# Moving the loads of the next tiles behind the read-back of rows, and the order of layer two's products, in a fused attention and mixture-of-experts kernel

## The chip, the cores and the metric

One NeuronCore of one Trainium2 chip runs the whole kernel. The metric is the device time of one execution in microseconds (us), taken as the median of several runs. A core has five instruction queues that matter here: TensorE (PE, matmuls and their weight loads), VectorE (DVE), ScalarE (ACT), GpSimd (POOL, which here only issues indirect DMAs) and SyncE (SP, which here only issues DMAs). Each queue runs its instructions in program order; an instruction that waits for a semaphore holds up all that stand behind it in its queue.

## The reference

```python
def attn(u, v, z):                       # u, v: (8, 2496, 256), z: (8, 2496, 64)
    scores = (1.0 / S) * (z @ z.transpose(0, 2, 1))
    return u * ((np.maximum(scores, 0.0) ** 2) @ v)

x = attn(u, v, z).reshape(19968, 256)
logits = x @ w_gate + modality_bias[modality_id]      # 8 experts
e_idx = logits.argmax(1)
gate_w = softmax(logits)[range(N), e_idx]
for e in range(8):                       # w1: (8, 256, 1024), w2: (8, 1024, 256)
    m = e_idx == e
    h = np.maximum(x[m] @ w1[e], 0.0)
    out[m] = gate_w[m, None] * (h @ w2[e])
```

## The kernel before

The first half of the time is the attention, which also computes each row's expert and scatters the rows to a DRAM buffer `xs`, sorted by expert. The second half is the mixture of experts, and only it is touched by the change. It works on tiles of 512 rows of one expert. There are 39 tiles that always run, numbered t = -4 to 34; t = -4 to -1 belong to one expert and share one set of weights, and from t = 0 on each tile reads its own expert's weights. Tiles -4 to 33 are "staged" (below); tile 34 and the rest after it take another path.

All products are made in float32r with operands split into a high and a low part, so that each product is three matmuls. A tile is computed in two halves of four slices of the hidden dimension (f = 0 to 3, then 4 to 7):

- `up` (L1356), for one slice f: six matmuls into one PSUM bank (L1365), then ACT writes the high part `hh` of the rectified result (L1369), and DVE the low part `hl` (L1370).
- `down` (L1434), after four `up`: 24 matmuls into two PSUM banks `po[0]` and `po[1]` (L1440). Sixteen take `hh` (with the high and the low part of the weights), and eight take `hl`.

So a tile is 96 matmuls of 128x512: 24 for four `up`, 24 for a `down`, and the same again. In `run_tile` the function `aside(f)` stands between these, and issues side work for other engines: after the first, second and fourth `up` and after the `down` of each half, as `aside(0)` to `aside(3)` and `aside(4)` to `aside(7)`.

The side work of a tile t is:

- Weights of tile t + 1. They arrive as four loads of 512 KB in buffers `wq` (L904); ACT casts each to a high part (L918) and DVE makes the low part (L922), one quarter in each of `aside(2)` to `aside(5)`. Seven buffers hold `wq`, so the last load for tile t + 2 needs the buffer that DVE's L922 of the first quarter of tile t + 1 reads.
- Rows of tile t + 1, which arrived as `xg` (four loads of 128 KB, L875) and `gate` (L877): DVE transposes them (`xt`, L941), ACT casts (`xh`, L948), DVE subtracts (`xl`, L953), in `aside(6)` and `aside(7)`. The second matmul of tile t + 1 reads `xl`.
- Results of tile t - 1. At the end of that tile `send` has DVE transpose the two banks (`squared`, L1452), and SP store them to a DRAM buffer (`stage`, L1456, four stores of 128 KB). The rest is put in a list `put_off`, with the step at which each is due: at `aside(2)` SP reads the tile back in another layout (`bring`, L1465, one load of 512 KB), and at `aside(4)`, `aside(5)`, `aside(6)` and `aside(6)` ACT multiplies a quarter of it by its gate (L1470), and POOL scatters that quarter to the output (L1389).

Loads for later tiles are issued on SP at the start of tile t, ahead of `run_tile(t)`: `prefetch(t)` issues the rows of tile t + 2 (L1632, which calls `fetch`, L859), and `fetch_weights(t + 2)` its weights (L1636, L890). SP's queue in a tile is therefore: the four stores of `stage` of the tile before, the rows of t + 2, the weights of t + 2, then `bring`.

Of the kernel before, what the change touches and what calls it, by code (L numbers as in the profile page):

```python
# [16 lines left out]
P = 128  # L17
# [5 lines left out]
def ins_of(x):  # L23
    return getattr(x, "ins", x)
# [3 lines left out]
def tile_attention_moe(ctx: ExitStack, tc: tile.TileContext, ut, v, zt, mid, wg, mb, w1, w2, out):  # L28
# [11 lines left out]
    nc = tc.nc  # L40
# [5 lines left out]
    KD, KF = D // P, F // P  # L46
# [9 lines left out]
    EARLY = min(4, (B - 1) * S // E // T)  # L56
    UNC = -(-N // T) - EARLY
# [51 lines left out]
    def iota_f32(shape, pattern, base, mult, name, pool=small):  # L109
        n = math.prod(shape[1:])  # L110
        i = raw.tile([P, n], I32, tag=name + "_i", name=name + "_i")
        f = pool.tile(shape, F32, name=name)
        nc.gpsimd.iota(i, pattern=pattern, base=base, channel_multiplier=mult)
        late.append((f, i))
        return f

    col = iota_f32([P, P], [[1, P]], 0, 0, "col", raw)
    part = iota_f32([P, 1], [[1, 1]], 0, 1, "part")
# [731 lines left out]
    def wait_rows(dmas):  # L850
        for s in scatters[ready["n"]:]:
            for i in dmas:
                tc.add_manual_dep(i, s.name, data, reason="rows of tokens")
        ready["n"] = len(scatters)

    def is_staged(t):
        return t < UNC - 1

    def fetch(t, r0=0, nj=J):  # L859

        n = t + EARLY
        cell = first[0:1, 1:2] if t < 0 else meta[0:1, t, 0:1]
        row = nc.sync.value_load(cell, min_val=0, max_val=(E - 1) * CAP if t < 0 else E * CAP - T)  # L863
        k = fetched["n"] % 2
        fetched["n"] += 1
        nt = nj * P
        xg = head[k].tile([P, T // BLK, KD * BLK], F32, tag=f"xg{k}", name="xg")[:, 0:nt // BLK, :]
        side = small.tile([P, J, 2], F32, tag="gate", bufs=4, name="gate")[:, 0:nj, :]
        r0 += n * T if t < 0 else 0
        src = xs[bass.ds(row + r0 if r0 else row, nt), :]  # L870
        dmas = []
        for b in range(P // BLK):
            cols = slice(b * KD * BLK, (b + 1) * KD * BLK)
            rows_of = src[:, cols].rearrange("(t i) c -> i t c", i=BLK)
            dmas.append(nc.sync.dma_start(out=xg[b * BLK:(b + 1) * BLK], in_=rows_of))  # L875
        order = "(p j) c -> p j c" if is_staged(t) else "(j p) c -> p j c"
        dmas.append(nc.sync.dma_start(out=side, in_=src[:, D:XW].rearrange(order, j=nj)))  # L877
        wait_rows([ins_of(i) for i in dmas])
        TL[t] = (side, xg)
# [7 lines left out]
    def weights_of(t):  # L887
        return W[0 if t < 0 else (t + 1) % NW]
# [27 lines left out]
    def part_weights_high(t, q):  # L916
        hi, _, x = quarter(t, q)
        nc.scalar.copy(out=hi, in_=x)  # L918

    def part_weights_low(t, q):  # L920
        hi, lo, x = quarter(t, q)
        nc.vector.tensor_tensor(out=lo, in0=x, in1=hi.bitcast(F32), op=ALU.subtract)  # L922
# [33 lines left out]
    def turn(t):  # L956
        for f in (turn_blocks, part_high, part_low):
            f(t)
# [20 lines left out]
    def piece(on, us, need, f, *args, after=(), take=(), drop=(), gate=-1):  # L979
        p = Piece(on, us, need, f, args, [d for d in (d if isinstance(d, tuple) else (d, 0.1) for d in after) if d[0]], list(take), drop, gate)  # L980
        pieces.append(p)
        return p
# [201 lines left out]
    for q in range(KD + 2):  # L1184
        h = piece("A", 0.95, G - 6 + q, part_weights_high, -1, q, after=[p])
        if q < KD:
            piece("D", 1.16, G - 5 + q, part_weights_low, -1, q, after=[h])
    x = piece("D", 1.16, G - 6, turn_blocks, -EARLY, after=[(p, -8.0)], take=[Hold("zm")])
    x = piece("A", 0.95, G - 5, part_high, -EARLY, after=[x], take=[Hold("zm"), Hold("zm")])
# [5 lines left out]
    with tc.manual_schedule(engines={ET.PE, ET.Activation, ET.DVE, ET.Pool, ET.SP}):  # L1195
# [33 lines left out]
        def ready_at(p):  # L1229
            t = 0.0  # L1230
            for d, lag in p.after:
                if d.start is None:
                    return None
                t = max(t, d.end + lag)
            return t
# [14 lines left out]
        while left:  # L1250
            e = min((e for e in clock if lists[e]), key=lambda e: clock[e])
            now = clock[e]
# [4 lines left out]
            for p in lists[e][:80]:  # L1257
                t = ready_at(p)
# [16 lines left out]
            if e == "Q":  # L1275
                for _ in range(p.issues):
                    now = max(now, landed[-LANES]) + 0.4
# [155 lines left out]

    def down(t, fs, h, po):  # L1434
        w = weights_of(t)[1]
        for part, sides in ((0, (0, 1)), (1, (0,))):
            for k in range(KD):
                for f in fs:
                    for q in sides:
                        nc.tensor.matmul(  # L1440
                            out=po[k], lhsT=w[:, f, q, k * P:(k + 1) * P], rhs=h[f][part],
                            start=f == q == part == 0, stop=f == KF - 1 and part == 1,
                        )

    put_off = []

# [80 lines left out]
    def turn_at(t):  # L1527
        return {-EARLY: 3, 1 - EARLY: 3, UNC - 1: 2}.get(t, KF - 2)

    def run_tile(t, ahead, extra={}, part="", beside=iter(()), kept=None):  # L1530
        if len(TL[t]) < 3:
            turn(t)
        staged = is_staged(t) and not part
        po = [ps_o.tile([P, 2 * D], F32, tag="o", name="po") for _ in range(KD if staged else TL[t][0].shape[1])]
        h = {}
        tiles = range(len(po))

        def aside(f):
            while put_off and put_off[0][0] <= f:
                put_off.pop(0)[1]()  # L1540
            q = f - 2 if kept is None else f - 1
            if ahead and t >= -1 and 0 <= q < KD + 2:
                part_weights_high(t + 1, q)
                part_weights_low(t + 1, q)
            for g in extra.get(f, ()):
                g()
            if ahead and t + 1 in TL:
                if f == turn_at(t):
                    turn_blocks(t + 1)
                if f == turn_at(t) + 1:  # L1550
                    part_high(t + 1)
                    part_low(t + 1)

        for f0 in range(0, KF, GROUP):
            fs = range(f0, f0 + GROUP)
            if f0 + GROUP == KF:
                for _ in range(2):
                    next(beside, None)
            for f in fs:
                h[f] = up(t, f)  # L1560
                if f == f0 or f == f0 + GROUP // 4:
                    aside(f)
                if f in (f0, f0 + 2) and f0 + GROUP == KF:
                    for _ in range(2 if f == f0 else 1):
                        next(beside, None)
            aside(f0 + GROUP // 2)
            if kept is not None and f0 + GROUP == KF:
                break
            if staged:
                down(t, fs, h, po)  # L1570
                aside(f0 + GROUP * 3 // 4)
                if f0 + GROUP == KF:
                    aside(KF)
                    aside(KF + 1)
                continue
            for f in fs:
                for j in tiles:
                    down_high(t, f, h, po, j)
                if f == f0 + GROUP * 3 // 4 - 1:
                    aside(f0 + GROUP * 3 // 4)  # L1580
                    if f0 + GROUP == KF:
                        aside(KF)
                        aside(KF + 1)
            if f0 + GROUP < KF:
                for j in tiles:
                    for f in fs:
                        down_low(t, f, h, po, j)
        next(beside, None)
        if staged:
            send(t, po)  # L1590
            return
        rows_out = finish(t, po, f"out{t}{part}", kept)
        for j in tiles:
            parts = (fs,) if kept is None else (fs[:-1], fs[-1:])
            for some in parts:
                if kept is not None:
                    for f in some:
                        down_high(t, f, h, po, j)
                for f in some:
                    down_low(t, f, h, po, j)  # L1600
            next(rows_out)
# [21 lines left out]
    planning = plan()  # L1623
# [4 lines left out]

    ph2.enter_context(tc.manual_schedule(engines={ET.PE, ET.Activation, ET.DVE, ET.Pool, ET.SP}))
    kept = []  # L1630
    for t in range(-EARLY, UNC):
        prefetch(t)  # L1632
        if t == 0:
            assert next(planning, planning) is planning
        if t >= 0 and t + 2 < min(UNC + 1, MAXT):
            fetch_weights(t + 2)  # L1636
        if t == UNC - 2 and MAXT > UNC:
            fetch(UNC, 0, 1)
        if t == UNC - 1 and MAXT > UNC:
            last = quarter_tile(UNC, "a", kept)  # L1640
            run_tile(t, True, between.get(t + EARLY, {}), beside=last, kept=kept)
        else:
            run_tile(t, t + 1 < min(UNC + 1, MAXT), between.get(t + EARLY, {}))
# [70 lines left out]
```

## Time and profile before

| | |
|---|---|
| median of 3 runs | 2348.11 us (2342.52 to 2356.02) |
| profiled execution | 2344.53 us |
| its span, first to last instruction | 2342.7 us |
| mean granted TensorE clock | 0.962 of 2.4 GHz |
| TensorE matmul busy | 2188.7 us, 93% of the span |
| VectorE, ScalarE busy | 1623.8 us (69%), 1446.9 us (62%) |
| mean DMA rate | 181 GB/s |

Busy time of PE is counted from each matmul's start to its modelled end, and matmuls overlap, so 93% does not say how fast they follow one another; the distance between starts does. The granted clock is the TensorE clock in parts of 2.4 GHz; it takes two values here, 1.0 and 0.5 (1.2 GHz). In the timeline, a row merges like instructions that follow one another: its start, its duration to the last one's end, how many (x), and in brackets how long the engine had been idle and what ended that.

### The profile page before, as it was taken

How to read it: one execution, taken by the hardware profiler on the slowest of the kernel's cores; microseconds unless marked ns; L12 is line 12 of the kernel's file. 1: busy time of each engine (PE TensorE's matmuls, PEld its weight loads, DVE VectorE, ACT ScalarE, POOL GpSimd, SP SyncE). 2: the span in 40 equal slices, each digit the busy share in tenths (PEclk: the TensorE clock that was granted, in tenths of full speed). 3: DMA queues.
4: the chain of work that ended last, by engine and by line, in shares of the span. 5: the costliest groups of instructions: out<-in, count | busy, mean ns of one | idle time of the engine just before them, and what ended most of it. 6: DMA issues, size and time to landing. Idle time of an engine off the chain costs nothing.

```text
span 2342.7 us, 44089 instructions
## 1 busy us (share of the span) xinstructions
PE 2188.7 (93%) x16582; PEld 1885.9 (81%) x16582; DVE 1623.8 (69%) x2363; ACT 1446.9 (62%) x2214; POOL 357.6 (15%) x342
## 2 busy tenths in 40 slices
PE   9999999999999999999999988888888888888885
PEld 7889998888888899999998766666666766666664
DVE  8888798898897898988976554444445554544443
ACT  8788788788887877878875343333344333433343
POOL 0000301203003021030240311111111111111112
PEclk9999999999999999999999998988999999989998
DMA  7977967879679687787783655555555555555551
GB/s 199 305 191 181 284 166 207 245 169 268 182 175 294 152 230 224 186 260 189 172 247 72 183 155 149 154 147 147 161 148 150 147 151 150 149 149 149 163 153 49
DMA packets 630121, 424.82 MB, mean 181 GB/s; under 512 B 216170, under 2 KB 579690, under 8 KB 629898
## 3 DMA queue, kind: packets, MB, share of 16 engines
q1 hardware_dynamic: 614810, 380.72, 60.1%
q0 software_dynamic: 15088, 41.21, 5.0%
q8 instruction: 131, 2.15, 0.4%
q14 instruction: 92, 0.75, 0.1%
HBM read 263.66 MB, written 158.13 MB: 180 GB/s over the span
## 4 chain that ended last, share of the span: by engine, by line
PE 70%; DMA 13%; ACT 6%; SPq 5%; issue 4%; DVE 1%; ACTq 0%; POOL 0%; POOLq 0%
PE acc L492 44%; PE po L1440 11%; DMA back<-stage 11%; PE s L343 7%; PE ph L1365 6%; ACT w L918 4%; DMA out_dram<-back,ids 2%; ACT hh L1369 2%; SPq L904 1%; PE po L596 1%; SPq L1456 1%; SPq L875 1%; DVE w L922 1%; ACT back L1470 1%; SPq L863 0%
## 5 line engine op out<-in xcount | busy, mean ns | idle before, releaser
L1440 PE MATMUL po<-hh,w 128*128 128x512 f32 x1216 | 370.8, 456 | 128.5 <-ACT hh L1369 128.5
L492 PE MATMUL acc<-ah,vh 64*128 64x512 f32 (+1 forms) x3120 | 460.7, 384 | 0.3 <-DVE ah L439 0.3
L492 PE MATMUL acc<-al,vh 64*128 64x512 f32 (+1 forms) x3120 | 450.2, 382 | 0.0
L492 PE MATMUL acc<-ah,vl 64*128 64x512 f32 (+1 forms) x3120 | 449.0, 382 | 0.0
L466 DVE TENSOR_TENSOR al<-r,ah 128x1024 fp32r<-128x1024 f32 (+4 forms) x514 | 431.7, 873 | 21.8 <-ACT ah L456 19.5
L1440 PEld LDWEIGHTS po<-hh,w 128*128 128x128 f32 x1216 | 266.5, 225 | 218.2 <-ACT hh L1369 160.9
L1369 ACT ACTIVATE hh<-ph 128x512 fp32r<-128x512 f32 x312 | 182.4, 596 | 407.0 <-PE ph L1365 407.0
L1365 PE MATMUL ph<-xh,w 128*128 128x512 f32 x1248 | 398.2, 390 | 0.0
L1370 DVE SCALAR_TENSOR_TENSOR hl<-ph,hh 128x512 fp32r<-128x512 f32 x312 | 211.7, 689 | 260.5 <-ACT hh L1369 260.3
L720 POOL DMA_INDIRECT xs<-x,sloti x160 | 197.2, 1232 | 1094.4 <-ACT ah L456 386.0
L492 PEld LDWEIGHTS acc<-al,vh 64*128 64x128 f32 x3120 | 333.0, 184 | 26.4 <-DVE al L470 0.8
L456 ACT CAST ah<-r 128x1024 fp32r<-128x1024 f32 (+5 forms) x475 | 333.7, 746 | 32.5 <-PE acc L492 22.8
L492 PEld LDWEIGHTS acc<-ah,vh 64*128 64x128 f32 x3120 | 327.9, 184 | 27.3 <-DVE ah L439 0.9
L492 PEld LDWEIGHTS acc<-ah,vl 64*128 64x128 f32 x3120 | 327.4, 184 | 26.8
L922 DVE TENSOR_TENSOR w<-wq,w 128x1024 fp32r<-128x1024 f32 x148 | 178.2, 1224 | 193.9 <-ACT w L918 193.8
L1389 POOL DMA_INDIRECT out_dram<-back,ids x152 | 150.9, 993 | 870.7 <-ACT back L1470 834.2
L1365 PEld LDWEIGHTS ph<-xh,w 128*128 128x128 f32 x1248 | 234.3, 188 | 49.0 <-PE acc L492 0.3
L356 ACT ACTIVATE r<-s 128x1024 f32<-128x1024 f32 (+2 forms) x206 | 209.4, 1018 | 85.6 <-PE s L343 68.3
L1365 PE MATMUL ph<-xl,w 128*128 128x512 f32 x624 | 242.9, 389 | 0.4 <-DVE xl L953 0.4
L432 ACT ACTIVATE r<-r 128x1024 f32<-128x1024 f32 (+2 forms) x205 | 215.6, 1052 | 5.4
L398 DVE STREAM_TRANSPOSE turn<-r 128x1024 f32<-128x1024 f32 x158 | 195.7, 1239 | 32.5 <-ACT r L432 25.2
L343 PE MATMUL s<-zm 64*128 64x512 f32 (+3 forms) x1452 | 204.0, 377 | 1.5 <-ACT r L356 1.5
(173 smaller groups left out, 1997.1 us busy)
## 6 DMA issues: line engine op xcount, KB each, us to landing
squares<-turn SPq DMA_DIRECT2D x632, 128.0 KB
r<-squares SPq DMA_DIRECT2D x158, 512.0 KB
wq<-in_moe_w_dram SPq DMA_DIRECT2D x148, 512.0 KB
ut<-in_ut_dram SPq DMA_DIRECT2D x40, 512.0 KB
xg<-xs SPq DMA_DIRECT2D x156, 128.0 KB
stage<-squared SPq DMA_DIRECT2D x152, 128.0 KB
back<-stage SPq DMA_DIRECT2D x38, 512.0 KB
vr<-in_v_dram SPq DMA_DIRECT2D x32, 512.0 KB
```

The source lines that it names most:

```text
L343: nc.tensor.matmul(out=s[t][:, w], lhsT=lhs, rhs=mv[halves[t], ql, w], start=n == 0, stop=n == 2)
L356: nc.scalar.activation(out=r[:, t, w], in_=s[t][:, w] if g < 2 else s[:, :, w], func=AF.Relu, scale=INV)
L432: nc.scalar.square(out=a[:, t, w], in_=r[:, t, w])
L456: copy(out=y, in_=x)
L466: nc.vector.tensor_tensor(out=y, in0=x, in1=h.bitcast(F32), op=ALU.subtract)
L492: nc.tensor.matmul(out=acc[b, c][r][dh][:, :w], lhsT=V[b, k // J][y][halves[r], k % J, dh * P:(dh + 1) * P], rhs=x[halves[r], t, :w], star ...
L720: nc.gpsimd.indirect_dma_start(out=xs, out_offset=bass.IndirectOffsetOnAxis(ap=RT[b]["sloti"][:n, k:k + 1], axis=0), in_=x[:n, j, :], in_o ...
L922: nc.vector.tensor_tensor(out=lo, in0=x, in1=hi.bitcast(F32), op=ALU.subtract)
L1365: nc.tensor.matmul(out=ph, lhsT=lhs, rhs=rhs[:, k, :], start=n == 0, stop=n == 3 * KD - 1)
L1369: nc.scalar.activation(out=hh, in_=ph, func=AF.Relu)
L1370: nc.vector.scalar_tensor_tensor(out=hl, in0=ph, scalar=0.0, in1=hh.bitcast(F32), op0=ALU.max, op1=ALU.subtract)
L1440: nc.tensor.matmul(out=po[k], lhsT=w[:, f, q, k * P:(k + 1) * P], rhs=h[f][part], start=f == q == part == 0, stop=f == KF - 1 and part == 1,)
```

## The change

`down` issues its sixteen matmuls on `hh` in another order. Before, all eight of `po[0]` stood ahead of all eight of `po[1]`; now the slices f come one after the other, and each slice's two matmuls into `po[0]` and two into `po[1]` stand together. The eight on `hl` keep their order.

The loads at the start of a tile (for t = 0 on) go to `put_off` with step 3, and so are issued in `aside(3)`, after the first `down` and after `bring`, which has step 2. `aside` now takes all entries of the list that are due, wherever they stand in it, so that the entries of steps 4 to 6, which `send` had put there earlier, do not hold back the new one. For t below 0 the loads are issued where they were.

```diff
     def down(t, fs, h, po):
         w = weights_of(t)[1]
-        for part, sides in ((0, (0, 1)), (1, (0,))):
-            for k in range(KD):
-                for f in fs:
-                    for q in sides:
-                        nc.tensor.matmul(
-                            out=po[k], lhsT=w[:, f, q, k * P:(k + 1) * P], rhs=h[f][part],
-                            start=f == q == part == 0, stop=f == KF - 1 and part == 1,
-                        )
+        terms = [(f, k, q, 0) for f in fs for k in range(KD) for q in range(2)]
+        terms += [(f, k, 0, 1) for k in range(KD) for f in fs]
+        for f, k, q, part in terms:
+            nc.tensor.matmul(
+                out=po[k], lhsT=w[:, f, q, k * P:(k + 1) * P], rhs=h[f][part],
+                start=f == q == part == 0, stop=f == KF - 1 and part == 1,
+            )
...
         def aside(f):
-            while put_off and put_off[0][0] <= f:
-                put_off.pop(0)[1]()
+            now = [x for x in put_off if x[0] <= f]
+            put_off[:] = [x for x in put_off if x[0] > f]
+            for x in now:
+                x[1]()
...
-    for t in range(-EARLY, UNC):
+    def order_loads(t):
         prefetch(t)
-        if t == 0:
-            assert next(planning, planning) is planning
         if t >= 0 and t + 2 < min(UNC + 1, MAXT):
             fetch_weights(t + 2)
         if t == UNC - 2 and MAXT > UNC:
             fetch(UNC, 0, 1)
+
+    for t in range(-EARLY, UNC):
+        if t == 0:
+            assert next(planning, planning) is planning
+        if 0 <= t:
+            put_off.append((3, lambda t=t: order_loads(t)))
+        else:
+            order_loads(t)
         if t == UNC - 1 and MAXT > UNC:
```

The first place is SP's queue over one tile in the middle of the second half. `stage` is the store of a finished tile and `back` its read-back, `xg` and `gate` are a tile's rows, and `wq` its weights; `stage_92` and `stage_93` are the two DRAM buffers that alternate. Before:

```order
L1456 DMA stage_92<-squared 32x16x64 x4
L863 TENSOR_LOAD meta
...
L875 DMA xg<-xs 32x16x64
...
L877 DMA gate<-xs 128x4x2
L893 TENSOR_LOAD meta
...
L904 DMA wq<-in_moe_w_dram 128x1024
L1465 DMA back<-stage_92 128x1024
L1456 DMA stage_93<-squared 32x16x64 x4
```

and with the change (line numbers after the edit are one lower in `send`):

```order
L1455 DMA stage_92<-squared 32x16x64 x4
L1464 DMA back<-stage_92 128x1024
L863 TENSOR_LOAD meta
...
L875 DMA xg<-xs 32x16x64
...
L877 DMA gate<-xs 128x4x2
L893 TENSOR_LOAD meta
...
L904 DMA wq<-in_moe_w_dram 128x1024
L1455 DMA stage_93<-squared 32x16x64 x4
```

The read-back now stands directly behind the four stores that it reads, and the nine loads of rows and weights stand behind it.

The second place is PE's queue in the `down` of a tile's second half, where `hh_25100`, `25118`, `25135` and `25146` are the high parts of slices 4 to 7, and `po_25018` and `25019` (now `24985` and `24986`) the two banks. Before:

```order
L1440 MATMUL po_25018<-hh_25100,w2_1_20158 128x512 x2
L1440 MATMUL po_25018<-hh_25118,w2_1_20158 128x512 x2
L1440 MATMUL po_25018<-hh_25135,w2_1_20158 128x512 x2
L1440 MATMUL po_25018<-hh_25146,w2_1_20158 128x512 x2
L1440 MATMUL po_25019<-hh_25100,w2_1_20158 128x512 x2
```

and with the change:

```order
L1439 MATMUL po_24985<-hh_25100,w2_1_20158 128x512 x2
L1439 MATMUL po_24986<-hh_25100,w2_1_20158 128x512 x2
L1439 MATMUL po_24985<-hh_25118,w2_1_20158 128x512 x2
L1439 MATMUL po_24986<-hh_25118,w2_1_20158 128x512 x2
L1439 MATMUL po_24985<-hh_25135,w2_1_20158 128x512 x2
L1439 MATMUL po_24986<-hh_25135,w2_1_20158 128x512 x2
L1439 MATMUL po_24985<-hh_25146,w2_1_20158 128x512 x2
```

The last slice's high part was needed by the seventh matmul and is now needed by the thirteenth.

## Rows read from the trace of the kernel before

**Rows 1.** The page's chain that ended last, by line, share of the span.
```profile
PE acc L492 44%; PE po L1440 11%; DMA back<-stage 11%; PE s L343 7%; PE ph L1365 6%; ACT w L918 4%; DMA out_dram<-back,ids 2%; ACT hh L1369 2%; SPq L904 1%; PE po L596 1%; SPq L1456 1%; SPq L875 1%; DVE w L922 1%; ACT back L1470 1%; SPq L863 0%
```
**Rows 2.** Busy time by stretch: attention, tiles 0 to 33; PEclk, DMA share, GB/s last.
```profile
0.00:1250.00 1250.00, 1247.14 (x12745) 1136.66 (x12746) 1074.59 (x1618) 1023.26 (x1543) 189.73 (x173) 1.00 0.79 213
...
1341.20:2290.60 949.40, 823.04 (x3266) 652.74 (x3264) 473.00 (x578) 373.08 (x578) 133.55 (x136) 0.92 0.52 151
```
**Rows 3.** Who waited for whom, 1341.2 to 2290.6: us, times, longest.
```profile
ACT back L1470 <- DMA back<-stage: 157.2, 34, 5.6
PE po L1440 <- ACT hh L1369: 126.4, 68, 3.7
```
**Rows 4.** Timeline of PE, the last eight products of some halves: start, us.
```profile
1302.43 1.98 PE L1440 MATMUL po<-hl,w 128*128 128x512 f32 x8
...
1324.19 1.98 PE L1440 MATMUL po<-hl,w 128*128 128x512 f32 x8
...
1339.39 1.99 PE L1440 MATMUL po<-hl,w 128*128 128x512 f32 x8
...
2288.74 1.98 PE L1440 MATMUL po<-hl,w 128*128 128x512 f32 x8
```
**Rows 5.** Timeline of PE, second half of one tile.
```profile
1721.07 0.39 PE L1365 MATMUL ph<-xh,w 128*128 128x512 f32 x1
...
1726.51 0.61 PE L1440 MATMUL po<-hh,w 128*128 128x512 f32 x2
1729.43 0.73 PE L1440 MATMUL po<-hh,w 128*128 128x512 f32 x2 [2.31 <-ACT hh L1369]
1731.27 4.45 PE L1440 MATMUL po<-hh,w 128*128 128x512 f32 x12 [1.10 <-ACT hh L1369]
```
**Rows 6.** Timeline of ACT, the same half.
```profile
1722.62 0.60 ACT L1369 ACTIVATE hh<-ph 128x512 fp32r<-128x512 f32 x1 [4.26 <-PE ph L1365]
1727.45 0.51 ACT L1470 ACTIVATE back<-back,gate 128x256 f32<-128x256 f32 x1 [4.22 <-DMA back<-stage]
```
**Rows 7.** Timeline of SP's DMA issues, the same tile.
```profile
1711.13 2.19 SPq L1456 DMA_DIRECT2D stage<-squared  x4
...
1717.93 2.35 SPq L904 DMA_DIRECT2D wq<-in_moe_w_dram  x4
1720.47 0.39 SPq L1465 DMA_DIRECT2D back<-stage  x1
```
**Rows 8.** Timeline of SP's DMA issues, tiles -3, -2 and 34.
```profile
1272.30 2.18 SPq L1456 DMA_DIRECT2D stage<-squared  x4
...
1278.38 0.55 SPq L1465 DMA_DIRECT2D back<-stage  x1
...
1304.20 0.35 SPq L1465 DMA_DIRECT2D back<-stage  x1
...
2292.51 2.69 SPq L1456 DMA_DIRECT2D stage<-squared  x4
```
**Rows 9.** Timeline of ACT, tiles -2 and 33: the first read-back quarter.
```profile
1307.82 0.51 ACT L1470 ACTIVATE back<-back,gate 128x256 f32<-128x256 f32 x1 [1.42 <-DMA back<-stage]
...
2282.03 0.51 ACT L1470 ACTIVATE back<-back,gate 128x256 f32<-128x256 f32 x1 [2.78 <-DMA back<-stage]
```
**Rows 10.** Timeline of PE, first matmuls of tile 34 and its first products of layer two.
```profile
2290.55 0.39 PE L1365 MATMUL ph<-xh,w 128*128 128x512 f32 x1
2291.31 0.50 PE L1365 MATMUL ph<-xl,w 128*128 128x512 f32 x1 [0.37 <-DVE xl L953]
2291.65 0.64 PE L1365 MATMUL ph<-xh,w 128*128 128x512 f32 x2
...
2296.70 3.79 PE L1376 MATMUL po<-w,hh 128*128 128x512 f32 x16
```
**Rows 11.** Timeline of PE, a second half at the lower clock.
```profile
1561.15 5.49 PE L1440 MATMUL po<-hh,w 128*128 128x512 f32 x12 [1.09 <-ACT hh L1369]
1566.44 2.32 PE L1440 MATMUL po<-hl,w 128*128 128x512 f32 x8
```

## The prediction

> **What bounds the kernel now.** I read the chain of waits first. TensorE carries most of it, but 11% of the span, some 258 us, lies on a DMA: `back<-stage`, the read-back of a finished tile [rows 1]. No other transfer has such a share, so I looked for the stretch in which it matters. By stretches, TensorE is filled in the attention (1247 of 1250 us busy, granted clock 1.00), while in tiles 0 to 33 it is busy for 823 of 949 us and the granted clock is 0.92 [rows 2]. The change is felt in this second stretch alone.
>
> Its list of waits names the cause: `po` waits 68 times, twice per tile, for ACT's `hh`, 126.4 us in all, and ACT waits 34 times, once per tile, for the read-back, 157.2 us [rows 3]. One tile shows how the two hang together. ACT finishes `hh` of slice 4 at about 1723.1 and then stands until 1727.45 at the first read-back quarter [rows 6]; behind it are the `hh` of slices 5, 6 and 7. TensorE has its `up` products done at 1726.51, makes two matmuls on slice 4, waits 2.31 us for slice 5, makes two, and waits 1.10 us more [rows 5]. The next twelve take 4.45 us from the first start to the last end, where full pace gives 11 × 0.2267 + 0.39 = 2.88: the clock fell after the pause. The reason for the lateness is on SP: the stores of `stage` go out at 1711.13, but the read-back is issued at 1720.47, behind all loads of rows and weights, and lands 7.0 us later [rows 6, 7].
>
> How long a tile would take without waits is seen before the stretch: two tile ends are 1324.19 − 1302.43 = 21.76 us apart [rows 4], 96 matmuls of 0.2267 us. In the stretch, 34 tiles take 2288.74 − 1339.39 = 949.35 us [rows 4], 27.92 each. The excess is 6.16 us per tile, 209.5 us in all. Of it 3.7 are the waits (126.4 / 34), most of the rest is the lower clock (8% of 949 us is 76, or 2.2 per tile).
>
> **The change, part by part.** *The loads behind the read-back.* Nothing is added; nine DMA issues per tile and two register loads move from ahead of the read-back to behind it. The read-back then waits only for the stores it reads. For that there are rows with little in the way. In tile -3 the stores began to be issued at 1272.30 and the read-back went out at 1278.38, 6.1 us later, with row loads in between; in tile -2 a read-back issued at 1304.20 with nothing ahead of it let ACT go at 1307.82, 3.6 us later [rows 8, 9]. The stores come 2.0 us after the tile's first matmul if DVE makes `xl` first (2290.55 to 2292.51 [rows 8, 10]). So the first quarter can be multiplied at +2.0 +6.1 +3.6 = +11.7 us in the tile. ACT comes to it after `hh` of slice 4: the fifth `up` starts 48 matmuls (10.9 us) into the tile, `hh` 1.55 us later (1721.07 to 1722.62 [rows 5, 6]), the quarter 0.5 after that, at +12.9. The read-back is there 1.2 us early, and the 157.2 us of ACT's waiting go.
>
> *What is late next.* ACT's and DVE's work behind the quarter stays as long as it is: quarters, two weight casts, three `hh`, then `xt`, `xh` and `xl` for the next tile. In tile 33 the quarter began at 2282.03, and the matmul that needs `xl` at 2291.31, 9.28 us on [rows 9, 10]. Put the quarter 0.49 us behind the start of that `hh`, and `xl` is usable 9.77 us after it. TensorE, no longer waiting, wants it sooner: from the fifth `up`'s first matmul, 49 matmuls or 11.11 us, less 1.55, is 9.56 us. So 0.21 us of waiting appear at the head of each tile, and the matmul after it was 0.34 instead of 0.23 us behind [rows 10]: 0.32 in all. As bounds I keep 0 (the list may close up) and the 0.64 us which tile 34 lost here (0.53 late, 0.11 slow). I take 0.32 since the chain is worked out from this very path. A tile is then 22.08 us.
>
> *The loads themselves* go out later: read-back at +8.1, rows next, first weights about 5 us on (1713.3 to 1717.93 in the old order [rows 7]), so at +13, the last by +15.5. All landed within 9.5 us of the first weight issue even with the read-back at their end (1717.93 to 1727.45 [rows 6, 7]), so by +22.5, and the next stores begin at +24. The weights' first cast is due after the next tile's fourth `up`, at 22.1 + 5.4 = +27.5, 5 us later. The buffer of the last load is free before +13, as its reader works right after slice 3. Cost nothing; if that cover were gone, ACT's casts would hold up `hh` as the quarters do now.
>
> *The order of the products.* Same 24 matmuls, same data. Slices 6 and 7 are needed at the ninth and thirteenth matmul instead of the fifth and seventh. TensorE went on with slice 6 3.82 us after the quarter's start (1727.45 to 1731.27 [rows 5, 6]); with the quarter in time that is 4.31 us after the start of `hh` of slice 4, and the old fifth matmul comes at 28 × 0.2267 − 1.55 = 4.80. So `hh` is in time in the old order too, and this part adds only slack: 0, up to 0.9 us (four matmuls) in a tile that still waits. What two banks in turn cost, the path after the staged tiles shows: sixteen `po` products that change the bank at each matmul take 3.79 us at full clock [rows 10], 3.40 + 0.39 for the last, so nothing. Taken alone it would gain little even now: with 16 matmuls left at 1731.27, TensorE would be through at 1734.9 and wait for `xl` until 1727.45 + 9.28 = 1736.7.
>
> *Sum.* 34 tiles at 21.76 plus 33 heads at 0.32 are 750.4 us, 199 us less than 949.35. Tile -1 keeps its loads where they were and may save 0.9 by the order. The profiled execution of 2344.5 us becomes 2344.5 − 199.0 − 0.9 = 2144.6. The median of the runs stands 3.6 us above that execution; I forecast **2148 us**, 8.5% less. A measurement of this kernel can tell about 0.5%, 12 us, from no change.
>
> **The rivals.** (1) *The read-back is still late, but less.* Weights and output scatters of one tile may still be moving when the next stores start, and then the read-back could take 7.0 us (1720.47 to 1727.45) instead of 3.6. It is ready at +15.1, 1.9 us after ACT gets there (12.9 plus the head's 0.32), and every us passes through to `xl`: 34 × 1.9 = 63, 2211 us. For it: a tile moves the same bytes in 22 instead of 28 us, so the mean DMA share of 0.52 [rows 2] rises to 0.66. Against: the sum of times above leaves the queue empty when the stores start.
>
> (2) *Slower: two banks in turn break the stream.* If the 32 products on `hh` of a tile ran as at the lower clock, 0.441 us each (1561.15 to 1566.44 for twelve [rows 11]), a tile would gain 6.86 us and lose 5.84, and 34 tiles would cost 35 us more: 2383 us. It decides from 0.41 us per matmul. Against stands the row with four banks in turn at full pace [rows 10]. The Trainium skill, "TensorE: Matmul & The Clock Gate", section "A second HAM failure mode: psum-queue depth-cycling", reports a kernel in which cycling through PSUM banks made the clock swing; by it the sum would be that of this rival, and the row here does not agree.
>
> (3) *Slower: the weights come too late.* From the first weight issue to the first cast there were about 26 us (issued 7.7 into the tile, due 5.4 into the next) and will be some 14.5. A wait there begins if the first load takes over 14.5 us, and at 20.3 (5.84 more) the gain is gone; at 22.3, 34 × 2 = 68 us are lost, 2416 us. All four took 9.5 us. The Trainium skill, "DMA: Bandwidth & Descriptors", section "Rules for kernel authors", advises to issue a DMA early and wait for it late. By that rule holding the loads back would be this rival; the trace differs, because here the early loads stand in front of one that is due sooner.
>
> (4) *No change*: SP's queue does not hold the read-back up after all, the stores do. Then 2348 us. The 9.3 us between store and read-back issue are filled with issues of loads, so I give it little. That the reordering is not carried out at all is excluded by the two orders shown ahead.
>
> **How the numbers follow.** The forecast with its bounds runs from all excess gone (2348.1 − 209.5 − 0.9 = 2138; less the 3.6 us by which the profiled execution stands under the median, 2134) to 2165 (a read-back late by half a us per tile); chance 0.74. Rival 1 from 2165 to 2250: 0.19. Rivals 2 and 3: 0.02 each, rival 4: 0.03. The range 2134 to 2205 holds the forecast and near half of rival 1. Faster by over 0.5%: 0.74 + 0.19 = 0.93; within: 0.03; slower: 0.04.
>
> **What would show it.** Right: per tile 22.1 us between ends; `back` issued about 8 us into the tile and ACT without a wait for it; `po` without waits for `hh`; granted clock 1.00 in this stretch; a short new wait of `ph` for `xl`, some 0.2 us, 33 times; DMA share near 0.66. Rival 1 would show ACT waiting 1 to 2 us per tile for `back`, and `ph` for `xl` by as much. Rival 2 would show distances over 0.23 us in the sixteen products on `hh`; rival 3 waits of ACT's L918 for `wq`. I am wrong in the main if tile ends stay over 25 us apart.

## The result and the profile after

| | before | after |
|---|---|---|
| median of the runs, us | 2350.15 (4 runs, 2342.52 to 2356.02) | 2146.12 (4 runs, 2145.53 to 2147.46) |
| profiled execution, us | 2344.53 | 2147.46 |
| its span, us | 2342.7 | 2145.7 |
| mean granted clock | 0.962 | 0.996 |
| TensorE busy | 93% | 99% |

The ratio is 0.9134, with an interval of 0.9107 to 0.9162: 8.7% less time. The forecast was 2148 us. (The median before is that of the three runs stated ahead and a fourth, taken with those of after.)

The chain that ended last, on the page of after, answers to [rows 1]:

```profile
PE acc L492 44%; PE ph L1365 13%; PE po L1439 10%; PE s L343 6%; DVE hl L1370 3%; DVE w L922 3%; DVE xl L953 2%; DMA out_dram<-back,ids 2%; DVE xt L941 2%; ACT xh L948 2%; ACT w L918 2%; PE po L596 2%; DMA squares<-turn 1%; SPq L416 1%; ACT back L1469 1%
```

`DMA back<-stage`, 11% before, is gone from it. In its place stands a chain of short pieces on ACT and DVE (`w`, `xt`, `xh`, `xl`), which leads to the head of the next tile. The busy times by stretch, in the columns of [rows 2], for the attention and for tiles 0 to 33:

```profile
0.00:1250.00 1250.00, 1246.32 (x12739) 1136.28 (x12740) 1073.70 (x1615) 1022.79 (x1542) 187.75 (x173) 1.00 0.79 213
1340.00:2093.50 753.50, 750.45 (x3266) 610.24 (x3265) 468.28 (x579) 369.82 (x579) 182.61 (x136) 1.00 0.68 190
```

The attention is as it was. The second stretch has as many matmuls (3266) in 753.5 instead of 949.4 us. Its granted clock rose from 0.92 to 1.00, and TensorE is without work for 3 us in all, where it was 126 before. The waits in the same stretch of after, in the columns of [rows 3]:

```profile
PEld ph L1365 <- DVE xl L953: 17.0, 34, 1.1
```

Both lines of [rows 3] are missing: ACT waits for no read-back, and `po` for no `hh`. New is a short wait of `ph` for `xl`, once per tile. The ends of the halves, to be held against [rows 4], with what the last half of tile -1 had ahead of its end:

```profile
1325.59 1.98 PE L1439 MATMUL po<-hl,w 128*128 128x512 f32 x8
...
1334.42 1.19 PE L1439 MATMUL po<-hh,w 128*128 128x512 f32 x4 [0.51 <-ACT hh L1369]
1336.25 2.12 PE L1439 MATMUL po<-hh,w 128*128 128x512 f32 x8 [0.63 <-ACT hh L1369]
1338.21 1.98 PE L1439 MATMUL po<-hl,w 128*128 128x512 f32 x8
...
1341.70 0.50 PE L1365 MATMUL ph<-xl,w 128*128 128x512 f32 x1 [0.76 <-DVE xl L953]
...
1361.58 1.98 PE L1439 MATMUL po<-hl,w 128*128 128x512 f32 x8
...
2091.68 1.98 PE L1439 MATMUL po<-hl,w 128*128 128x512 f32 x8
```

From these the difference of the two spans, 197.0 us, is put together. The end of 1324.19 came 1.4 us later, at 1325.59. The half of tile -1 that follows took 1338.21 − 1325.59 = 12.62 instead of 15.20 us, 2.6 less. Tiles 0 to 33 took 2091.68 − 1338.21 = 753.47 instead of 949.35 us, 195.9 less. What follows them stayed as long (54.0 us). From the start of tile 0's last eight products on, 33 tiles take 2091.68 − 1361.58 = 730.10 us, 22.12 each; tile 0 takes 23.37, since its head has to wait for `xl` until 1341.70: in tile -1 the read-back is still late, and it delays all that follows on ACT and DVE.

One tile in the middle of after: first its head, in the timeline of PE.

```profile
1518.23 0.39 PE L1365 MATMUL ph<-xh,w 128*128 128x512 f32 x1
1518.69 0.50 PE L1365 MATMUL ph<-xl,w 128*128 128x512 f32 x1
1519.03 0.64 PE L1365 MATMUL ph<-xh,w 128*128 128x512 f32 x2
```

SP's DMA issues in the same tile, against [rows 7]:

```profile
1519.88 2.20 SPq L1455 DMA_DIRECT2D stage<-squared  x4
1524.51 0.34 SPq L1464 DMA_DIRECT2D back<-stage  x1
...
1529.40 2.02 SPq L904 DMA_DIRECT2D wq<-in_moe_w_dram  x4
```

And ACT at its first quarter of the read-back, against [rows 6]:

```profile
1531.57 0.50 ACT L1469 ACTIVATE back<-back,gate 128x256 f32<-128x256 f32 x1
```

The tile starts at 1518.23. Its second matmul comes 0.46 us after the first and the third 0.34 after that, where full pace is 0.2267 each: 0.35 us lost, and nothing else in the tile. The read-back goes out 4.6 us after the first store, where it was 9.3 before. The quarter starts 13.34 us into the tile without a wait, where ACT had waited 4.22 us before.

### The profile page after: what moved, and what is told of

Its sections match the earlier page's. It is cut to its first block, busy times and chain, and to the rows that moved or that the text cites. A ratio compares the mean times of both kernels' runs of the same rounds, so it can differ in the third digit from the quotient of the medians.

```text
span 2145.7 us, 44124 instructions
## 1 busy us (share of the span) xinstructions
PE 2115.1 (99%) x16582; PEld 1842.8 (86%) x16582; DVE 1617.1 (75%) x2363; ACT 1443.2 (67%) x2214; POOL 404.4 (19%) x342
## 4 chain that ended last, share of the span: by engine, by line
PE 75%; DVE 11%; ACT 5%; DMA 4%; issue 3%; SPq 1%; POOL 0%; ACTq 0%; POOLq 0%; DVEq 0%
PE acc L492 44%; PE ph L1365 13%; PE po L1439 10%; PE s L343 6%; DVE hl L1370 3%; DVE w L922 3%; DVE xl L953 2%; DMA out_dram<-back,ids 2%; DVE xt L941 2%; ACT xh L948 2%; ACT w L918 2%; PE po L596 2%; DMA squares<-turn 1%; SPq L416 1%; ACT back L1469 1%
## 5 line engine op out<-in xcount | busy, mean ns | idle before, releaser
L1389 POOL DMA_INDIRECT out_dram<-back,ids x152 | 199.8, 1314 | 623.0 <-ACT w L918 557.0
L1439 PE MATMUL po<-hh,w 128*128 128x512 f32 x1216 | 288.6, 389 | 1.1 <-ACT hh L1369 1.1
L1439 PEld LDWEIGHTS po<-hh,w 128*128 128x128 f32 x1216 | 228.1, 188 | 49.2 <-ACT hh L1369 2.0
L922 DVE TENSOR_TENSOR w<-wq,w 128x1024 fp32r<-128x1024 f32 x148 | 178.2, 1223 | 33.0 <-ACT w L918 32.9
```

The lines of the kernel that those rows point to most:

```text
L1389: nc.gpsimd.indirect_dma_start(out=out, out_offset=bass.IndirectOffsetOnAxis(ap=ids[:, j:j + 1], axis=0), in_=y, in_offset=None, bounds_ch ...
L1439: nc.tensor.matmul(out=po[k], lhsT=w[:, f, q, k * P:(k + 1) * P], rhs=h[f][part], start=f == q == part == 0, stop=f == KF - 1 and part == 1,)
```

## The experiments

The main theory: the read-back is late because nine loads stand ahead of it in SP's queue; ACT, waiting for it, holds up `hh`; TensorE, waiting for `hh`, loses time twice, in the pause and by the clock. The rivals: the order of the products is what gained; it is the moment of the loads and not their place in the queue; the loads' moving does something else (contention). Nine kernels were run, all of which compute the whole reference. Each median is of four runs, and each ratio is to the kernel before on the same chip. The medians of the kernel before in these ratios are 2345.95 us (first four rows), 2348.81 (next four) and 2346.03 (last), so differences of 2 to 4 us between kernels are read from their traces and not from the medians.

| kernel | median us | ratio (interval) |
|---|---|---|
| order of the products alone | 2322.80 | 0.9890 (0.9865 to 0.9916) |
| loads alone | 2148.82 | 0.9151 (0.9129 to 0.9174) |
| rows' loads early, weights' late | 2147.03 | 0.9146 (0.9123 to 0.9168) |
| weights' loads early, rows' late | 2248.45 | 0.9584 (0.9554 to 0.9613) |
| the same in the old order | 2268.89 | 0.9672 (0.9623 to 0.9722) |
| read-back first, loads at the tile's start | 2142.41 | 0.9129 (0.9094 to 0.9163) |
| after, rows turned one step earlier | 2133.81 | 0.9089 (0.9055 to 0.9123) |
| loads ahead as before, gates late | 2130.60 | 0.9079 (0.9045 to 0.9113) |
| last three together | 2131.04 | 0.9080 (0.9063 to 0.9098) |

### The two parts apart

*The order alone* is before with only the first piece of the diff (that in `down`).

> Only the new order of the products; the loads stay ahead of the read-back. Main theory (the place of the loads carries the gain, the order is slack): ACT still waits over 3 us per tile for the read-back, and the next tile's low rows sit in the same late chain. A lower bound of the period is the loop read-back quarter to xl (9.28 us), to the stores (1.2), to the read-back's issue (9.34), to its landing (7.0): 26.8 us against 27.92, so at most 38 us are gained: 2310 to 2345 us, likeliest 2325. Rival (the order carries a good part, since it removes the second wait of each tile and with it the fall of the clock): 2250 us or less.

It took 2322.80 us, 23 less than before. The waits of the stretch 1345 to 2090 us:

```profile
ACT back L1469 <- DMA back<-stage: 132.7, 27, 6.6
PE po L1439 <- ACT hh L1369: 78.4, 45, 4.3
PE ph L1365 <- DVE xl L953: 7.9, 17, 0.8
```

ACT still waits for the read-back, 4.9 us a time (before 157.2 / 34 = 4.6), so the cause is untouched. `po` waits 78.4 / 27 = 2.9 us a tile instead of 3.7. A part of that comes back at the next head, which now waits for `xl`: it is made at the end of the same late chain on ACT and DVE. By its timeline of PE the 34 tiles take 27.33 us each instead of 27.92, 20 us in all, and tile -1 another 2.5 us less. In 31 of the 34 tiles the clock still fell behind the pause, as in the first two of these rows; in three, one of them the last two rows, the products kept full pace:

```profile
1500.80 1.31 PE L1439 MATMUL po<-hh,w 128*128 128x512 f32 x4 [2.64 <-ACT hh L1369]
1502.63 3.78 PE L1439 MATMUL po<-hh,w 128*128 128x512 f32 x8 [0.52 <-ACT hh L1369]
...
1528.14 1.19 PE L1439 MATMUL po<-hh,w 128*128 128x512 f32 x4 [1.62 <-ACT hh L1369]
1529.97 2.10 PE L1439 MATMUL po<-hh,w 128*128 128x512 f32 x8 [0.64 <-ACT hh L1369]
```

Eight products take 3.78 us in the one and 2.10 in the other. So the granted clock stays low, as the busy times from 1345 to 2080 us say (columns as in [rows 2]):

```profile
1345.00:2080.00 735.00, 648.61 (x2584) 507.04 (x2585) 370.57 (x458) 296.07 (x459) 106.28 (x108) 0.93 0.54 155
```

*The loads alone* is after with `down` as it was.

```diff
-        terms = [(f, k, q, 0) for f in fs for k in range(KD) for q in range(2)]
-        terms += [(f, k, 0, 1) for k in range(KD) for f in fs]
-        for f, k, q, part in terms:
...
+        for part, sides in ((0, (0, 1)), (1, (0,))):
+            for k in range(KD):
+                for f in fs:
+                    for q in sides:
...
```

> Only the new place of the loads; the products in the old order. Main theory: the read-back is in time, hh of slices 6 and 7 are ready some 0.4 us before the old order needs them, so 2146 us, within 6. Rival (the order is needed as well): waits of po for hh come back in each tile, 2180 us or more.

It took 2148.82 us, 2.7 more than after. The stretch behind tile -1 has no wait of `po` for `hh` here either. The difference lies in tile -1, whose loads the change leaves where they were, so that its `hh` is late. Its timeline of PE:

```profile
1335.17 0.73 PE L1440 MATMUL po<-hh,w 128*128 128x512 f32 x2 [1.51 <-ACT hh L1369]
1337.00 5.49 PE L1440 MATMUL po<-hh,w 128*128 128x512 f32 x12 [1.10 <-ACT hh L1369]
1342.29 2.35 PE L1440 MATMUL po<-hl,w 128*128 128x512 f32 x8
```

The last of these rows against the same one of after (1338.21) shows what the old order does to a half with late `hh`: it pauses 2.61 instead of 1.14 us, and its twelve products then follow at (1342.29 − 1337.00) / 12 = 0.44 us, the distance of the lower clock in [rows 11]. That half takes 3.9 us longer than in after, and tile 0, whose head then waits less, 1.2 us less. So the loads carry nearly all of the gain. With the loads moved, the new order is worth 2.7 us and not the 23 that it brings by itself: both act on the same waits, and tile -1 alone still has them.

### Which loads, and what about them

*Rows early*: after, but only the weights' loads are put off, the rows' loads go out at the tile's start.

```diff
     def order_loads(t):
-        prefetch(t)
...
         if t == 0:
             assert next(planning, planning) is planning
+        prefetch(t)
```

> The changed kernel, but the loads of rows go back ahead of the read-back; those of weights stay behind it. Main theory: the read-back is issued no later than now, since it waits for the stores for about as long as the row loads take to issue, and lands up to 1 us later, inside the slack: 2146 to 2160 us. Rival (any load ahead of the read-back makes it late, rows as much as weights): 2200 us or more.

2147.03 us, the same as after (2146.12) within 1 us. SP's issues show that the rows go out in a time in which the read-back has to wait for its stores anyway (in after it goes out 4.6 us after the first store with nothing between):

```profile
1518.51 2.19 SPq L1455 DMA_DIRECT2D stage<-squared  x4
1521.78 1.93 SPq L875 DMA_DIRECT2D xg<-xs  x4
...
1524.80 0.40 SPq L1464 DMA_DIRECT2D back<-stage  x1
```

The read-back goes out 6.3 us after the first store, 1.7 later than in after, and still in time. It is the weights that had to go.

*Weights early* is the opposite: the rows' loads are put off, and the weights' loads stand ahead of the read-back.

```diff
     def order_loads(t):
         prefetch(t)
-        if t >= 0 and t + 2 < min(UNC + 1, MAXT):
-            fetch_weights(t + 2)
...
         if t == 0:
             assert next(planning, planning) is planning
+        if t >= 0 and t + 2 < min(UNC + 1, MAXT):
+            fetch_weights(t + 2)
```

> The changed kernel, but the loads of weights go back ahead of the read-back; those of rows stay behind it. Main theory: the 2 MB of weights in front of the read-back make it late by about 2.4 us beyond what the tile hides, each us passes on to the next tile's low rows: 2190 to 2260 us, likeliest 2228. Rival (the row loads, with their many small packets and register loads, were the delay): 2150 us.

2248.45 us: half of the gain is gone. It is 20 us above the likeliest value. The waits of the stretch 1345 to 2090 us name the place, first those of the engines:

```profile
ACT back L1469 <- DMA back<-stage: 83.5, 30, 4.5
```

and in the same stretch those of SP's own queue:

```profile
SPq L904 <- DVE w L922: 61.0, 30, 2.3
```

The last weights' load needs a buffer that DVE frees in mid-tile. Issued so early it waits 2.0 us for that, 30 times, with the read-back behind it. The kernel before had this wait 16 times for 6.2 us in all (SP's waits, 1345 to 2285 us); there the rows' loads stood ahead of the weights'. The expectation had left it out; that it is the whole of the 20 us was not tried.

*Weights early, in the old order* is that kernel with `down` as in the kernel before.

> The weights' loads ahead of the read-back as in the run before, 2248 us, with the products in the old order: what the order is worth while ACT is late by 2 to 3 us. In that run the pauses of TensorE were split in four of at most 0.8 us (two in the products, two at the next tile's head) and the clock stayed up. Main theory: in the old order they fall together into one stretch of the half and the clock falls in most tiles; but the chain to xl, not TensorE, sets the period, so only what outlasts that chain shows: 2248 to 2275 us, likeliest 2258. Rival (the order is slack in every state): 2248 us within 6; other rival (the clock's fall adds in full, 1.5 us per tile): 2290 us or more.

2268.89 us, 20 more. The two kernels, the same stretch of each (columns as in [rows 2]), first that with the new order:

```profile
1345.00:2080.00 735.00, 674.53 (x2829) 525.04 (x2828) 404.30 (x500) 322.39 (x499) 113.78 (x116) 1.00 0.63 169
```

and that with the old:

```profile
1345.00:2080.00 735.00, 668.08 (x2751) 524.76 (x2749) 394.73 (x486) 314.53 (x488) 111.57 (x114) 0.97 0.62 166
```

The granted clock is 1.00 with the new order and 0.97 with the old one. A second half of a tile in each, again the new order first, by the timeline of PE:

```profile
1486.65 1.19 PE L1439 MATMUL po<-hh,w 128*128 128x512 f32 x4 [0.63 <-ACT w L918]
1488.48 2.11 PE L1439 MATMUL po<-hh,w 128*128 128x512 f32 x8 [0.65 <-ACT hh L1369]
...
1493.93 0.50 PE L1365 MATMUL ph<-xl,w 128*128 128x512 f32 x1 [0.76 <-DVE xl L953]
```

and two of the old order:

```profile
1386.39 0.73 PE L1440 MATMUL po<-hh,w 128*128 128x512 f32 x2 [1.34 <-ACT hh L1369]
1388.22 3.04 PE L1440 MATMUL po<-hh,w 128*128 128x512 f32 x12 [1.10 <-ACT hh L1369]
...
1462.38 0.73 PE L1440 MATMUL po<-hh,w 128*128 128x512 f32 x2 [1.34 <-ACT hh L1369]
1464.20 4.63 PE L1440 MATMUL po<-hh,w 128*128 128x512 f32 x12 [1.10 <-ACT hh L1369]
```

The new order splits the lateness into pauses at the products and at the next head. The expectation put each at 0.8 us or less; most are, and the longest was 2.1. Behind them the products kept full pace in 33 of the 34 tiles. The old order has nearly the whole lateness at the products, and the twelve behind the pauses took about 4.6 us in 16 of the 34 tiles and 3.0 to 3.1 in the other 18. The two tiles shown have the same two pauses, one with the clock up and one with it down, so the length of the pauses by itself does not tell when the clock falls; what else decides was not found. The lower clock costs 16 × 1.6 = 25 us by these rows, an estimate that is as large as the whole difference of 20 us. So where ACT waits 2 to 3 us for the read-back, the new order is worth 20 us, and by this estimate what it saves is the clock. Where ACT waits 4.9 us, as with the order alone, the new order does not keep the clock up (0.93).

*Read-back first, loads at the tile's start*: before with the new order, and the read-back issued at once by `send` instead of being put in the list. SP's queue has the order of after, but the loads are where they were in the program.

```diff
-        put_off.append((2, bring))
+        bring()
```

> The loads are ordered at the start of the tile as before, but the read-back is ordered ahead of them, right behind its stores; the new order of products. Main theory (only the order on SP's queue counts, since SP runs ahead of the other engines): SP's queue is then the same as in the changed kernel, and so is the time, 2146 us within 6. Rival (the loads have to come in mid-tile): 2200 us or more.

2142.41 us. So it does not matter that the program names the loads at the start of the tile and not in its middle. SP's issues show why:

```profile
1519.62 0.34 SPq L1464 DMA_DIRECT2D back<-stage  x1
...
1524.57 2.02 SPq L904 DMA_DIRECT2D wq<-in_moe_w_dram  x4
```

The weights go out 5.0 us behind the read-back, in after 4.9, and the read-back waits for its stores in both. For that reason this kernel cannot tell the loads' place in SP's queue from the moment at which they go out; the kernel with late gates, below, can. It is 3.7 us faster than after. Of that 2.9 are seen in the timelines of PE, since tile -1 is helped as well: the last products of its halves start at 1323.61 and 1334.49 here, 10.88 us apart without a pause, where after takes 12.62, and tile 0 takes 22.16 us where after takes 23.37.

### What was left, and another way to the same end

*Rows turned one step earlier*: after, with `xt`, `xh` and `xl` of the next tile made one step earlier.

```diff
-        return {-EARLY: 3, 1 - EARLY: 3, UNC - 1: 2}.get(t, KF - 2)
+        return {-EARLY: 3, 1 - EARLY: 3, UNC - 1: 2}.get(t, KF - 3)
```

> The changed kernel, with DVE's transpose of the next tile's rows one step earlier, ahead of hl of slices 6 and 7. Main theory (what is late next is xl, by 0.35 us at the head of each tile, since DVE comes to the transpose only after two hl): xl is ready about 0.8 us before TensorE wants it, tiles take 21.76 instead of 22.12 us, 34 x 0.36 = 12 us less: 2134 us, 2130 to 2139. Rival (the 0.35 us come from something else, or the two hl now hold up layer two's last products): 2144 us or more.

2133.81 us, 12.3 less than after: 33 heads at 0.35 us are 11.6. By the busy times from 1345 to 2080 us TensorE has no gap any more:

```profile
1345.00:2080.00 735.00, 735.00 (x3244) 608.82 (x3243) 469.53 (x575) 368.46 (x576) 212.21 (x136) 1.00 0.70 194
```

In its timeline of PE the sixteen products on `hh`, which change the bank at every second one, run at full pace:

```profile
1487.52 3.79 PE L1439 MATMUL po<-hh,w 128*128 128x512 f32 x16
...
2056.90 1.98 PE L1439 MATMUL po<-hl,w 128*128 128x512 f32 x8
...
2078.66 1.98 PE L1439 MATMUL po<-hl,w 128*128 128x512 f32 x8
```

A tile takes 2078.66 − 2056.90 = 21.76 us, the 96 matmuls and nothing else.

*Gates late*: before with the new order and its loads ahead of the read-back, as they were; only ACT's four multiplications by the gate are put off, to the step behind the tile's last product. If the DMA itself were what TensorE waits for, this could not help.

```diff
-        put_off.extend((min(4 + j, 6), lambda j=j: put(j)) for j in range(J))
+        put_off.extend((8 if t < UNC - 2 else min(4 + j, 6), lambda j=j: put(j)) for j in range(J))
```

> The loads stay ahead of the read-back as in the kernel before, so that it lands as late as before, and the multiplication by the gates is moved behind xh in ACT's queue, to the end of the tile; the new order of products. Main theory (the late read-back costs time only because hh of slices 5 to 7 stand behind it in ACT's queue): the wait goes though the read-back is as late, 2130 to 2155 us, likeliest 2137 as two quarters leave the chain to xl. Rival (the late transfer itself, its traffic or what waits on it elsewhere, is what costs): 2250 us or more.

2130.60 us, the fastest. SP's issues in a tile:

```profile
1511.77 2.60 SPq L1455 DMA_DIRECT2D stage<-squared  x4
...
1519.66 2.01 SPq L904 DMA_DIRECT2D wq<-in_moe_w_dram  x4
1521.85 0.43 SPq L1464 DMA_DIRECT2D back<-stage  x1
```

and ACT in its timeline, at the end of a tile:

```profile
1508.13 1.05 ACT L948 CAST xh<-xt 128x1024 fp32r<-128x1024 f32 x1 [2.24 <-DVE xt L941]
1509.09 1.71 ACT L1469 ACTIVATE back<-back,gate 128x256 f32<-128x256 f32 x4
```

The read-back is issued 10.1 us after the first store, later still than before (9.3 [rows 7]). It costs nothing now, since nothing urgent stands behind it on ACT; and without quarters between the `hh`, `xl` is ready for the head too. Hence neither the loads' early issue nor the read-back's late one costs time by itself. What cost it was an instruction on ACT that waited for its data in front of `hh`, and this can be cured at either end. (Late gates with the old order of products were not run.)

*All three*: after's order of products, the read-back first, the rows a step earlier and the gates late.

> All three cures together: the read-back ahead of the loads, the transpose of the next rows one step earlier, the gates behind xh. Main theory (with either of the last two, tiles -1 to 33 already run at TensorE's own pace of 21.76 us, so that nothing is left for another cure): 2130 us, within 5, the same as with the late gates alone. Rival (some waiting was left that the traces hide): 2120 us or less.

2131.04 us, no less than gates late alone: a tile takes 21.76 us here as well, and TensorE has nothing left to give in this stretch.

## Why the prediction was right

- *What bounded the kernel* held: the runs that free ACT of the wait, by SP's queue (2142.41, 2146.12, 2147.03, 2148.82) or by ACT's own order (2130.60), all end within 19 us of one another, and the one that leaves it (order alone) keeps 2322.80.
- *The tile*: forecast 22.08 us, measured 22.12. The head, 0.32, measured 0.35; the first quarter at +13.2 (12.9 and the head), measured +13.34, and without a wait.
- *The read-back* was issued at +6.3, not +8.1. The stores began at +1.65 instead of +2.0, and the 6.1 us between stores and read-back came from tile -3, where row loads stood between; with nothing between it is 4.6. The error was on the safe side, since ACT came to the quarter only at +13.3.
- *The loads themselves* cost TensorE nothing: the weights went out at +11.2 (forecast +13), and ACT's L918 has no wait for `wq` in the stretch. The DMA share is 0.68, forecast 0.66.
- *The order* was put at nothing beyond slack, up to 0.9 us in a waiting tile. In tile -1 it gave 2.7 us net (after against loads alone). What fell short is that the 0.9 us counted the four matmuls' slack and not the clock: in that tile the twelve products behind the pause take 5.49 us in the old order, and run at full pace in the new. "Alone it would gain little" held, at 23 us or 1%, though not at nothing. With 20 us between the two weights-early kernels this is the one term of the reasoning that was mis-sized; in after only tile -1 still waits for `hh`, so the sum did not show it.
- *Sum*: forecast −199.0 for the tiles and −0.9 for tile -1, measured −195.9 and −2.6; the 3.1 us in the first are tile 0's head (23.37 − 21.76 = 1.6) and 33 tiles at 22.124 instead of 22.08 (1.45). That the median agrees to 2 us is in part luck: the profiled execution took 2147.46 us, 2.9 more than the forecast 2144.6, and the median lies 1.3 us under it and not 3.6 above.
- *Rival 1*, a read-back still late: not seen. Made to happen (weights early), it cost 102 us, 3.0 per tile at an ACT wait of 83.5 / 30 = 2.8 us, so that every us did pass through to the tile, as that rival had it. Its price had a slip: 34 × 1.9 is 65 us, not 63; nothing else hangs on it.
- *Rival 2*, two banks in turn: fell. Sixteen products that change the bank take 3.79 us, as [rows 10] had it for four banks, and the clock is 1.00. The swing of the clock that the Trainium skill reports of a kernel that cycles through PSUM banks, in "TensorE: Matmul & The Clock Gate", section "A second HAM failure mode: psum-queue depth-cycling", does not happen here.
- *Rival 3*, weights too late: fell, no such wait. The advice of the Trainium skill, "DMA: Bandwidth & Descriptors", section "Rules for kernel authors", to issue a DMA early and wait for it late, is borne out in its second half by the kernel with late gates (2130.60 us). Its first half fails where the early DMA stands in a queue ahead of one that is due sooner (weights early, 102 us over after).

## What to carry to other kernels

When an engine waits for a DMA, look at what stands ahead of that DMA in its issuing queue, and at what stands behind the waiting instruction on its engine: sort the queue by due time, or move the consumer to where nothing urgent is behind it. Here the first brought 8.5% by itself, and the second, one line beside the new order of products, 9.2%. Where operands may come some us late, order the products so that each operand is consumed as late as the sums allow: with the weights early, that kept the granted clock at 1.00 instead of 0.97 and was worth 20 us, while with a wait of 4.9 us (order alone) it did not keep the clock up and was worth 23.

## What the runs showed of the hardware

POOL's issue of an output scatter takes longer in after. The lines give the group of these issues in tiles 0 to 33; the number behind the busy time is the mean ns of one. Before:

```profile
L1389 POOL DMA_INDIRECT out_dram<-back,ids x136 | 133.5, 982 | 817.4 <-ACT back L1470 805.1 <-issue 10.1 <-ACT xh L948 2.2
```

After:

```profile
L1389 POOL DMA_INDIRECT out_dram<-back,ids x136 | 182.6, 1343 | 570.4 <-ACT w L918 538.2 <-issue 20.4 <-ACT hh L1369 10.4
```

The kernel with late gates has 973 ns there. What DVE does at the same time decides. In one tile of after the first scatter takes 1.87 us and the third 0.97, by the timeline of POOL:

```profile
1533.24 1.87 POOL L1389 DMA_INDIRECT out_dram<-back,ids  x1 [15.90 <-ACT w L918]
...
1537.25 0.97 POOL L1389 DMA_INDIRECT out_dram<-back,ids  x1 [0.30 <-issue]
```

and by that of DVE:

```profile
1533.04 1.22 DVE L922 TENSOR_TENSOR w<-wq,w 128x1024 fp32r<-128x1024 f32 x1 [0.57 <-ACT w L918]
```

The first scatter begins while DVE's L922 is running and ends 0.85 us after it (1535.11 against 1534.26). In after, 69 of the 136 scatters begin while DVE runs L922 or L953, both of which read two tiles in SBUF. Each of these takes 1.5 us or more and ends 0.83 to 0.86 us after DVE's instruction. The other 67 take 0.97 or 0.98 us, also those that begin beside a transpose or an `hl`. Before, one of 136 begins so, and it alone is long. With the rows turned one step earlier, where the loads go out as in after, L953 runs at the start of the fourth scatter of a tile, and that one too becomes long (101 of 136 in 1345 to 2080 us). So the loads in flight are not the cause: the issue waits for DVE's instruction. What the two engines share is not shown here. It costs nothing in these kernels, as no engine waits for POOL.
